# Bands of 192 keys from the second group's pairs on, and the seventh group's second product as seven of quarters

## The chip, the cores and the metric

One Trainium2 chip, one of its cores. The metric is the device time of one execution in microseconds (us), lower is better. The core has a matrix engine (TensorE: PE in the profile, its weight loads PEld), VectorE (DVE), ScalarE (ACT), GpSimd (POOL) and a queue that issues DMA transfers (SyncE: SP).

## The reference

```python
def _attn_ref(q, k, v):                       # 8 batches, 8 heads, 576 positions, 64 wide
    window = 128
    scores = scale * np.matmul(q, k.transpose(0, 1, 3, 2))
    bias = slopes[:, None, None] * (-np.abs(rel).astype(np.float32))[None, :, :]
    mask = (rel >= 0) & (rel < window)
    scores = np.where(mask, scores + bias[None], -1000000000.0)
    scores = scores - np.max(scores, axis=-1, keepdims=True)
    attn = np.exp(scores)
    attn = attn / (np.sum(attn, axis=-1, keepdims=True) + 1e-09)
    return np.matmul(attn, v).astype(np.float32)

def _moe_ref(x, w_in, w_out):                 # 4608 tokens, 512 wide, 2048 hidden
    h = x @ w_in
    g = h * (1.0 / (1.0 + np.exp(-h)))
    return (g @ w_out).astype(np.float32)
```

A query sees itself and the 127 keys before it. The output of attention, its heads side by side, goes through two dense layers with a SiLU between them.

## The kernel before

**Tiles.** The 4608 tokens are 36 tiles of 128, and four tiles are one of nine groups of 512 (numbered 0 to 8; the seventh is group 6). Attention works in 72 **pairs**: pair p is tile p // 2 with half of the heads (four of them). Two batches make nine tiles, so that in every ninth tile (block 0) there are no earlier keys.

**A pair** goes through `scores` (TensorE, queries times keys), `other_batch` (a fill where a tile spans two batches), `row_max` (VectorE: scores plus the bias table `tab`, and the row's extreme), `exps` (ScalarE), `p_hi` and `p_lo` (the weights as two fp16 parts in a buffer `hr`, made by ScalarE and by GpSimd or VectorE), `p_transpose` (DMA transposes from `hr` to `hl`), `attend` (TensorE, weights times values) and `normalize`, `x_hi`, `x_lo`. Queries of a tile reach 128 keys of the tile before and 128 of their own. `banded(p)` says how the keys are cut. Not banded, all 128 queries are multiplied with all 256 keys. Banded, the first 64 queries take the first 192 keys of the 256, the last 64 queries the last 192, so each row has 192 scores (`WIN`). Before, pairs 36 to 71 are banded; their queries and keys are fp16 in two parts, three products for each score. Pairs 8 to 35 are not banded, and their queries and keys are fp32. Pairs 0 to 7 belong to group 0 and run ahead of the dense layers.

**The dense layers.** Each group has 16 steps n (n = 16 times the group, plus f). A step has a first product (`gemm1`, tag h), the activation in parts `act1` (ScalarE), `act2` (VectorE), `act3` (ScalarE) and `act4` (VectorE), and a second product (`gemm2`, tag o). From group 2 on, all operands are fp16 in two parts, three matmuls for each product. Groups in `FAST` take the second product as seven products of quarters (`gemm2_fast`, tag m) in place of eight: for each step `act_sums` makes three more sums of quarters of the activation, and `act3` and `act4` then work on seven quarters in place of four. The sums of weights that this needs are made on GpSimd far ahead (`SUM_WORK`); from step 120 on the first product is made of sevens too (`gemm1_seven`), with sums of the first weights (`IN_WORK`), kept in DRAM meanwhile. When half of a fast group is through, `join_products` adds the products up and stores the result. Before, FAST holds groups 7 and 8.

**The order.** It is written by hand. A step has four positions: the two halves of `gemm1` and the two halves of an earlier step's `gemm2` (how much earlier says `lag_of`: one step in groups 0 to 5, rising to three towards a fast group, three and four in it). At each position `begin()` runs what `put`, `later` and `ahead` have planned for it, so the place of each instruction on its engine is fixed when the kernel is built. `at(p)` gives the position of a pair's scores, 7 apart from pair 18 on; `attend` follows 11 to 19 positions later. Engines work down their own queues in order.

**Buffers.** Not banded, each half of a pair takes one of two `hr` buffers. Banded, all pairs share one buffer (`room`, with gaps of zeros that `clear_room` sets once), and two transposes send it out when both halves are in it. PSUM gives two banks to tag h, two to tag a (scores, attend), and one each to w, x, y, z (second product).

Of the kernel before, what the change touches and what calls it, by code (L numbers as in the profile page):

```python
# [117 lines left out]
SUM_TAGS = tuple(f"w1_{k}" for k in range(7, 15))  # L118
# [34 lines left out]
def tile_window_attention_then_silu_mlp(ctx, tc, qk, v, w_in, w_out, distance, out):  # L153
# [212 lines left out]
    def rescale_bias(b):  # L366

        ratio = vsc[b][:, 8:9] if b > QK16 else vsc[b][:, 7:8]
        for s in range(2):
            off = HALF * s if b == QK16 else 0  # L370
            nc.vector.tensor_scalar_mul(
                tab[halves[s], :, :WIN], tab[halves[s], :, off : off + WIN], ratio[halves[s]]
            )
# [249 lines left out]
    def split_of(p, u, what):  # L623
        if banded(p):
            parts = what[:, HALF:].rearrange("p (u a h c) -> p u a h c", u=2, a=2, h=2)
            return parts[:, u, :, :, :WIN]
        n = 2 - blocks(p).start
        return what[:, : 4 * n * P].rearrange("p (a h c) -> p a h c", a=2, h=2)

    def p_hi(p, u):  # L630
        t, n = st[p]["t"][u], (2 - blocks(p).start) * P
        if banded(p):
            st[p]["hr", u] = hr = room[0]
            nc.scalar.copy(split_of(p, u, hr)[:, 0], t)  # L634
            return
# [1044 lines left out]
```

## Time and profile before

| | us |
|---|---|
| median of 3 runs (897.73 to 897.88) | 897.84 |
| the profiled execution | 896.72 |
| its span, first to last instruction | 894.9 |
| PE busy | 886.3 (99%) |
| DVE busy | 647.4 (72%) |
| ACT busy | 589.1 (66%) |
| POOL busy | 418.5 (47%) |

Busy time of a matmul contains a modelled end, and matmuls overlap. What a stretch of matmuls costs is therefore read below from the start of one stretch to the start of the next, not from the busy time of its instructions. An fp32 matmul of scores leaves two records in the trace, an fp16 one a single record.

### The profile page before, as it was taken

To read this page: it belongs to the slowest core of one execution; us is meant where nothing else is said; L and a number is where in the kernel's file an instruction comes from. 1 tells how busy PE (TensorE), PEld (TensorE's weight loads), DVE (VectorE), ACT (ScalarE), POOL (GpSimd) and SP (SyncE) were. 2 spreads that over 40 slices of the span, in tenths; PEclk is the share of its full clock that TensorE was granted. 3 is DMA by queue.
4 is the path that set the end of the run, shared out by engine and by line. 5 is a ranking of instruction groups with operands and counts; after the bars stand their busy time and mean duration, and the time that the engine had idled before them with its cause. 6 is when DMAs were issued, how large, how long until landed. Compare 5 with 4: busy or idle time off the path is not lost.

```text
span 894.9 us, 22095 instructions
## 1 busy us (share of the span) xinstructions
PE 886.3 (99%) x8617; PEld 589.6 (66%) x8617; DVE 647.4 (72%) x1654; ACT 589.1 (66%) x1321; POOL 418.5 (47%) x494
## 2 busy tenths in 40 slices
PE   9999999999999999999999999999999999999998
PEld 7877777888855555445455554445555568899997
DVE  6997988678876766655777667575776659776665
ACT  7789987776578855777765555565566554465653
POOL 2356651112112211666676776686777412443441
PEclk9999999999999999999999999999999999999999
DMA  8979925345588744869885557565575455400000
GB/s 322 399 191 263 244 56 134 72 95 96 117 216 220 191 96 119 179 163 225 188 155 108 109 105 154 123 118 109 125 166 95 84 85 142 142 26 13 14 25 26
DMA packets 207193, 123.22 MB, mean 138 GB/s; under 512 B 170864, under 2 KB 173040, under 8 KB 207088
## 3 DMA queue, kind: packets, MB, share of 16 engines
q1 hardware_dynamic: 206656, 121.41, 56.7%
q8 instruction: 68, 1.11, 0.5%
q10 hardware_dynamic: 432, 0.39, 0.1%
q14 instruction: 37, 0.30, 0.1%
HBM read 66.72 MB, written 13.63 MB: 90 GB/s over the span
## 4 chain that ended last, share of the span: by engine, by line
PE 79%; DVE 8%; ACT 5%; DMA 3%; POOL 3%; issue 2%; SPq 1%; DVEq 0%; POOLq 0%; ACTq 0%
PE o L1248 26%; PE h L1032 22%; PE m L1151 7%; PE h L1037 5%; PE sp L535 4%; PE av L713 4%; PE h L975 3%; PE hb L975 3%; PE sp L556 2%; PE av L699 1%; ACT t L613 1%; DMA qs<-qk 1%; SPq L664 1%; DMA vm<-v 1%; PE pt L678 1%
## 5 line engine op out<-in xcount | busy, mean ns | idle before, releaser
L1032 PE MATMUL h<-xt,w 128*128 128x512 f16 (+1 forms) x1344 | 269.0, 349 | 0.0
L1248 PE MATMUL o<-w,gb 128*128 128x512 f16 x960 | 224.4, 379 | 0.8 <-DVE gb L1120 0.6
L1032 PEld LDWEIGHTS <-w 128*128 128x128 f16 x1344 | 126.6, 98 | 111.7 <-issue 3.3
L1071 DVE SCALAR_TENSOR_TENSOR h<-gt,h 128x512 f32<-128x512 f32 x112 | 77.6, 693 | 127.2 <-ACT gt L1065 126.6
L1248 PEld LDWEIGHTS <-gb 128*128 128x128 f16 x960 | 90.2, 98 | 104.9 <-DVE gb L1120 2.6
L1065 ACT ACTIVATE gt<-h,tsc 128x512 f32<-128x512 f32 x104 | 71.1, 683 | 112.7 <-PE h L1032 105.2
L202 POOL TENSOR_TENSOR hr<-t,hr 128x384 f16<-128x384 f32 (+2 forms) x54 | 55.9, 1036 | 127.7 <-ACT hr L634 64.4
L202 POOL TENSOR_TENSOR x<-xs,x 128x256 f16<-128x256 f32 x54 | 37.3, 690 | 160.3 <-ACT x L752 151.1
L1248 PE MATMUL o<-w,gh 128*128 128x512 f32 x256 | 82.9, 405 | 0.1
L1106 ACT ACTIVATE gb<-h 128x512 f16<-128x512 f32 x80 | 47.4, 592 | 35.5 <-DVE h L1071 35.2
L613 ACT ACTIVATE t<-t,mx,vsc 128x192 f32<-128x192 f32 x144 | 69.0, 537 | 1.2
L1120 DVE SCALAR_TENSOR_TENSOR gb<-h,gb 128x512 f16<-128x512 f32 x80 | 54.8, 685 | 18.7 <-ACT gb L1106 18.6
L613 ACT ACTIVATE t<-t,mx 128x256 f32<-128x256 f32 (+1 forms) x144 | 61.8, 488 | 3.6 <-DVE mx L598 2.7
L713 PEld LDWEIGHTS <-hl 128*128 128x128 f16 x1464 | 51.8, 98 | 14.6 <-issue 3.9
L713 PE MATMUL av<-v,hl 128*128 128x65 f16 (+1 forms) x1464 | 54.9, 193 | 0.1
L1083 POOL TENSOR_TENSOR gt<-gt 128x256 f32<-128x256 f32 x27 | 21.4, 794 | 68.5 <-DVE gt L1074 68.5
L1248 PEld LDWEIGHTS o<-w,gh 128*128 128x128 f32 x256 | 45.6, 188 | 10.0 <-issue 0.5
L598 DVE CUSTOM_DVE_ANT_0 t<-sp,tab 128x256 f32<-128x256 f32 (+1 forms) x144 | 50.1, 402 | 1.9 <-PE sp L535 1.7
L1248 PE MATMUL o<-w,gl 128*128 128x512 f32 x128 | 50.7, 396 | 0.2
L980 ACT COPY hs<-h 128x128 f32<-128x128 f32 x72 | 19.0, 264 | 41.7 <-PE h L975 38.9
L204 DVE SCALAR_TENSOR_TENSOR hr<-t,hr 128x384 f16<-128x384 f32 (+2 forms) x54 | 42.8, 792 | 5.0 <-ACT hr L634 3.8
L202 POOL TENSOR_TENSOR w<-wm,w 128x512 fp32r<-128x512 f32 x32 | 43.7, 1366 | 2.5
(236 smaller groups left out, 1835.2 us busy)
## 6 DMA issues: line engine op xcount, KB each, us to landing
qs<-qk SPq DMA_DIRECT2D x18, 512.0 KB, 4.6
r<-qk SPq DMA_DIRECT2D x18, 512.0 KB, 4.5
wr<-w_in SPq DMA_DIRECT2D x16, 512.0 KB, 6.5
wr<-w_out SPq DMA_DIRECT2D x16, 512.0 KB, 6.2
rv<-v SPq DMA_DIRECT2D x30, 256.0 KB, 3.6
out<-ot SPq DMA_DIRECT2D x28, 256.0 KB, 2.4
vm<-v SPq DMA_DIRECT2D x27, 256.0 KB, 4.4
q<-qk SPq DMA_DIRECT2D x18, 256.0 KB, 3.4
```

Source lines behind the costliest of these rows:

```text
L202: engine.tensor_sub(out, a, b)
L598: nc.vector.tensor_tensor_reduce(out=st[p]["t"][u][:, h, 2 * P - n :], in0=st[p]["sp"][h][:, u, o].rearrange("p o c -> p (o c)"), in1=tab[ ...
L613: nc.scalar.activation(x, x, AF.Exp, bias=mx[:, 2 * u + h : 2 * u + h + 1], scale=scale)
L713: nc.tensor.matmul(av[:, 2 * u + h, : rhs.shape[-1]], lhs, rhs, start=(n == 0), stop=(n == len(seq) - 1), skip_group_check=True,)
L975: nc.tensor.matmul(h[to], w_of(j, w, a, cc), x_of(g, t, x, b, cc), start=w in ("11", "S1") and i == 0, stop=i == len(terms) - 1, skip_grou ...
L1032: nc.tensor.matmul(o, w[:, wp, cc], x, start=start and k == 0, stop=stop, skip_group_check=True)
L1065: nc.scalar.activation(gt, hps[n], AF.Tanh, scale=scale)
L1071: nc.vector.scalar_tensor_tensor(out=h, in0=gt, scalar=1.0, in1=h, op0=ALU.add, op1=ALU.mult)
L1106: nc.scalar.activation(gh, gt, AF.Copy, scale=cut_of(n))
L1120: nc.vector.scalar_tensor_tensor(out=gl, in0=gt, scalar=cut_of(n), in1=f32(gh) if n // NF < OUT16 else gh, op0=ALU.mult, op1=ALU.subtract)
L1151: nc.tensor.matmul(product(k), a[:, k], sum_part(k, j, part), start=j == 0 and side == 0 and a is gh and part == 0, stop=n == last and a i ...
L1248: nc.tensor.matmul(ops[ti], a[:, t], w, start=(f == 0 and i == 0), stop=(f == NF - 1 and i == len(seq) - 1), skip_group_check=True,)
```

## The change

1. `banded(p)` holds from pair 8 on. `scores_banded` gets a form with a single fp32 product for pairs 8 to 35. `row_max`, `exps`, `p_hi`, `p_lo`, `p_transpose` of these 28 pairs work on 192 keys; all share the one `hr` buffer, which is cleared at the start (position -18), and `p_transpose` is called once a pair. The bias table is shifted for the second half of the queries by a copy of its own (`shift_bias`, position -16) and no longer when it is first rescaled.
2. `FAST` holds group 6 too. Its `act_sums` run on GpSimd, two positions after `act2` (`SUM_LATE`). Its first product is cut into matmuls of 256 columns, as in the other fast groups. The lag of three steps is reached in group 5.
3. The GpSimd work on sums of weights starts earlier and runs denser (`SUMS` 172 in steps of 25; it was 200 in steps of 28), so that it ends before group 6.
4. Places: pairs 10 to 14 one or two positions later (`CLOSE`), the attends of pairs 21 to 35 at 18 positions behind the scores, of pairs 9 to 17 one position sooner, `act3` and `act4` of group 7 one position later, sums of group 7 on GpSimd from step 114 (was 116). Buffers: the cleared buffer has the tag hr, the joined sums of group 7 and 8 take their turn in it.

```diff
-SUMS, SUMS_STEP = 200, 28
+SUMS, SUMS_STEP = 172, 25
-HR_CLEAR = 150
+HR_CLEAR = -18
+SHIFT = -16
-FAST = (NG - 2, NG - 1)
+FAST = (NG - 3, NG - 2, NG - 1)
-CLOSE = (-6, 5, 8, 14, 20, 26, 32, 38)
+CLOSE = (-6, 5, 10, 15, 21, 27, 32, 38)
...
     def banded(p):
-        return p >= 2 * QK16 * NBLK
+        return p >= 2 * GT
...
-                for n, (a, b) in enumerate(((0, 0), (1, 0), (0, 1))):
+                terms = ((0, 0), (1, 0), (0, 1)) if i >= QK16 * NBLK else ((None, None),)
+                for n, (a, b) in enumerate(terms):
...
+                            lhs = qs[i][rows, 2 * q + u, halves[s]] if a is None else q16[i][rows, a, 2 * q + u, halves[s]]
+                            rhs = ks[k][rows, 2 * q + u, keys] if a is None else k16[k][rows, b, 2 * q + u, keys]
                             nc.tensor.matmul(
-                                sp[h][halves[s], u, at4 : at4 + keys.stop - keys.start],
-                                q16[i][rows, a, 2 * q + u, halves[s]], k16[k][rows, b, 2 * q + u, keys],
-                                start=n == 0, stop=n == 2, skip_group_check=True,
+                                sp[h][halves[s], u, at4 : at4 + keys.stop - keys.start], lhs, rhs,
+                                start=n == 0, stop=n == len(terms) - 1, skip_group_check=True,
                             )
...
-        st[p]["hr", u] = hr = pool.tile([P, 8 * P], F16, tag="hr", bufs=2, name=f"hr{p}_{u}")
...
-        nc.sync.dma_start_transpose(hl[:, : 4 * n], hr[:, : 4 * n * P])
...
-        act_sums(n)
+        if n >= ALONE * NF or not SUM_LATE:
+            act_sums(n)
...
+                            if g in FAST and g < ALONE and SUM_LATE:
+                                ahead(1 + SUM_LATE, act_sums, n)
```

The rows below stand as the two programs have them, engine by engine. First TensorE at pair 20, in group 1: sp is the scores, k the keys of the earlier and of the own tile, q the queries. Before, the whole pair:

```order
L535 MATMUL sp_0_2483<-k_1582,q_2016 128x128
L535 MATMUL sp_1_2484<-k_1582,q_2016 128x128
L535 MATMUL sp_0_2483<-k_2018,q_2016 128x128
L535 MATMUL sp_1_2484<-k_2018,q_2016 128x128
L535 MATMUL sp_0_2483<-k_1582,q_2016 128x128
L535 MATMUL sp_1_2484<-k_1582,q_2016 128x128
L535 MATMUL sp_0_2483<-k_2018,q_2016 128x128
L535 MATMUL sp_1_2484<-k_2018,q_2016 128x128
```

TensorE at the same place in the changed kernel, half of the pair (the other half reads the same):

```order
L563 MATMUL sp_0_2559<-k_1637,q_2082 64x128
L563 MATMUL sp_1_2560<-k_1637,q_2082 64x128
L563 MATMUL sp_0_2559<-k_2084,q_2082 64x128
L563 MATMUL sp_1_2560<-k_2084,q_2082 64x128
L563 MATMUL sp_0_2559<-k_2084,q_2082 64x64
L563 MATMUL sp_1_2560<-k_2084,q_2082 64x64
L563 MATMUL sp_0_2559<-k_1637,q_2082 64x64
L563 MATMUL sp_1_2560<-k_1637,q_2082 64x64
```

Eight matmuls of 128 queries and 128 keys became sixteen of 64 queries and 128 or 64 keys. Next TensorE in the second product of step 101 in group 6 (gb: the activation's two parts, w: a weight, o: an output tile). Before, one half of its 12 matmuls:

```order
L1248 LDWEIGHTS gb_9899
L1248 MATMUL o_0_9543<-w_1_2_3479,gb_9899 128x512
L1248 LDWEIGHTS gb_9899
L1248 MATMUL o_0_9543<-w_1_2_3479,gb_9899 128x512
L1248 LDWEIGHTS gb_9899
L1248 MATMUL o_0_9543<-w_1_2_3479,gb_9899 128x512
```

TensorE in the changed kernel, the same step, the first six of its 21 matmuls (m: a bank with two products, ws: sums of weights, gt: the activation's first part):

```order
L1141 LDWEIGHTS gt_10292
L1141 MATMUL m_0_1_9890<-w_1_6_4338,gt_10292 128x256
L1141 LDWEIGHTS gt_10292
L1141 MATMUL m_0_1_9890<-w_1_6_4338,gt_10292 128x256
L1141 LDWEIGHTS gt_10292
L1141 MATMUL m_0_1_9890<-w_1_2_3565,gt_10292 128x256
L1141 LDWEIGHTS gt_10292
L1141 MATMUL m_0_1_9890<-w_1_2_3565,gt_10292 128x256
L1141 LDWEIGHTS gt_10292
L1141 MATMUL m_0_3_9895<-ws_7753,gt_10292 128x256
L1141 LDWEIGHTS gt_10292
L1141 MATMUL m_0_3_9895<-ws_7753,gt_10292 128x256
```

Twelve matmuls of 512 columns became 21 of 256. Last GpSimd in group 6, from pair 64's p_lo on (hr) to the next pair's (x: attention's output in two parts, v: values, wr, wq, ws: sums of weights). Before:

```order
L202 TENSOR_TENSOR hr_0_4009<-t_0_9695,hr_0_4009 128x2x192
L807 TENSOR_TENSOR wr_9728<-w_1_7_4364 128x512
L816 TENSOR_TENSOR wq_9851<-wr_9728 128x256
L817 TENSOR_TENSOR wq_9851<-wr_9728 128x256
L202 TENSOR_TENSOR x_9871<-xs_9773,x_9871 128x256
L504 TENSOR_SCALAR v_69<-rv_9703,vsc_7153 128x8x64
L819 TENSOR_TENSOR wq_9851<-wr_9728 128x256
L820 TENSOR_TENSOR wq_9851<-wr_9728 128x256
L834 CAST ws_9891<-wq_9851 128x2x256
L822 TENSOR_TENSOR wr_9728<-wr_9728 128x256
```

GpSimd in the changed kernel, the same pair on (gt: sums of the activation's quarters):

```order
L207 TENSOR_TENSOR hr_0_528<-t_0_9972,hr_0_528 128x2x192
L1073 TENSOR_TENSOR gt_10016<-gt_10016 128x256
L1074 TENSOR_TENSOR gt_10016<-gt_10016 128x256
L1075 TENSOR_TENSOR gt_10016<-gt_10016 128x128
L207 TENSOR_TENSOR x_10193<-xs_10076,x_10193 128x256
L1073 TENSOR_TENSOR gt_10115<-gt_10115 128x256
L1074 TENSOR_TENSOR gt_10115<-gt_10115 128x256
L1075 TENSOR_TENSOR gt_10115<-gt_10115 128x128
L508 TENSOR_SCALAR v_69<-rv_9983,vsc_7382 128x8x64
L207 TENSOR_TENSOR hr_0_528<-t_0_10187,hr_0_528 128x2x192
```

The sums of weights are gone from group 6, and three sums for each step stand in their place.

## Rows read from the trace of the kernel before

**Rows 1.** The page: span, busy time by engine.

```profile
span 894.9 us, 22095 instructions
...
PE 886.3 (99%) x8617; PEld 589.6 (66%) x8617; DVE 647.4 (72%) x1654; ACT 589.1 (66%) x1321; POOL 418.5 (47%) x494
```

**Rows 2.** Who TensorE waited for: us in total, times, longest.

```profile
PE warm L224 <- POOL ident masks.py:199: 1.3, 1, 1.3
PE hb L975 <- DMA wy<-away: 0.6, 2, 0.4
...
PE pt L678 <- ACT t L613: 0.3, 1, 0.3
```

**Rows 3.** TensorE in time order: start us, busy us, line, shapes, records. fp32 pairs.

```profile
149.35 0.71 PE L535 MATMUL sp<-k,q 64*128 64x128 f32 x8
149.99 1.27 PE L1032 MATMUL h<-xt,w 128*128 128x256 f16 x10
...
228.87 1.16 PE L535 MATMUL sp<-k,q 64*128 64x128 f32 x16
229.96 1.48 PE L1032 MATMUL h<-xt,w 128*128 128x256 f16 x12
```

**Rows 4.** TensorE in time order: an fp16 banded pair.

```profile
374.39 0.72 PE L556 MATMUL sp<-packed,packed 64*64 64x128 f16 x48
375.04 2.76 PE L1248 MATMUL o<-w,gb 128*128 128x512 f16 x12
```

**Rows 5.** TensorE in time order: fp32 matmuls 65 columns wide.

```profile
29.13 3.68 PE L699 MATMUL av<-vf,hl 128*128 128x65 f32 x32
32.65 1.92 PE L767 MATMUL xp<-ident,early 128*128 128x128 f32 x16
```

**Rows 6.** TensorE in time order: a second product in group 6.

```profile
646.81 2.75 PE L1248 MATMUL o<-w,gb 128*128 128x512 f16 x12
649.40 0.88 PE L713 MATMUL av<-v,hl 128*128 128x65 f16 x24
```

**Rows 7.** TensorE in time order: first and second product in group 7.

```profile
754.15 0.60 PE L1151 MATMUL m<-w,gt 128*128 128x256 f16 x4
...
756.44 2.78 PE L1004 MATMUL h<-xt,w 128*128 128x256 f16 x24
759.06 0.60 PE L1151 MATMUL m<-w,gh 128*128 128x256 f16 x4
```

**Rows 8.** Windows, groups 0 and 6: length, busy PE, PEld, DVE, ACT, POOL, clock, DMA.

```profile
35.60:146.60 111.00, 110.64 (x754) 86.60 (x752) 96.23 (x239) 95.78 (x210) 60.45 (x62) 1.00 0.73 195
640.90:728.50 87.60, 87.60 (x973) 44.49 (x971) 57.72 (x153) 51.95 (x106) 49.06 (x56) 1.00 0.57 115
```

**Rows 9.** VectorE by line and shape, 652 to 747 us: busy us, mean ns, idle.

```profile
L1120 DVE SCALAR_TENSOR_TENSOR gb<-h,gb 128x512 f16<-128x512 f32 x14 | 9.6, 685 | 2.5 <-ACT gb L1106 2.4
```

**Rows 10.** VectorE and GpSimd by line and shape, 775 to 880 us.

```profile
L1113 DVE SCALAR_TENSOR_TENSOR gl<-gt,gh 128x640 f16<-128x640 f32 x12 | 9.9, 823 | 0.0
L1113 DVE SCALAR_TENSOR_TENSOR gl<-gt,gh 128x256 f16<-128x256 f32 x12 | 6.6, 548 | 0.0
L1083 POOL TENSOR_TENSOR gt<-gt 128x256 f32<-128x256 f32 x22 | 16.5, 752 | 55.4 <-DVE gt L1074 55.4
...
L1085 POOL TENSOR_TENSOR gt<-gt 128x128 f32<-128x128 f32 x23 | 12.8, 558 | 1.8
```

**Rows 11.** VectorE and GpSimd in time order, group 7: start us, busy us.

```profile
762.58 0.84 POOL L1083 TENSOR_TENSOR gt<-gt 128x256 f32<-128x256 f32 x1 [2.96 <-DVE gt L1074]
762.76 2.21 DVE L1113 SCALAR_TENSOR_TENSOR gl<-gt,gh 128x640 f16<-128x640 f32 x2
763.38 1.30 POOL L1084 TENSOR_TENSOR gt<-gt 128x256 f32<-128x256 f32 x1
```

**Rows 12.** DMA issues, 40 to 100 us, and ScalarE's wait on them, 36 to 150 us.

```profile
hl<-hr SPq DMA_TRANSPOSE x12, 3.6
...
ACT hr L638 <- DMA hl<-hr: 2.1, 2, 1.7
```

More of the change, by code (lines that the diff above doesn't have):

```diff
@@ L117 @@
 OUT_TAGS = {3: ("q", 2), 4: ("q", 2), 5: ("q", 2), 6: ("q", 2)}
[L118 removed]
+SUM_TAGS = tuple(f"w1_{k}" for k in (7, 8, 9, 14, 10, 11, 12, 13))
 MORE_TAGS = (("w1_15", 1), ("k", KSLOTS), ("k", KSLOTS))
@@ L368, in rescale_bias, with shift_bias @@
         ratio = vsc[b][:, 8:9] if b > QK16 else vsc[b][:, 7:8]
[L369 to L373, printed above, removed]
+        nc.vector.tensor_scalar_mul(tab[:, :, :WIN], tab[:, :, :WIN], ratio)
+    def shift_bias():
+        nc.vector.tensor_copy(tab[halves[1], :, :WIN], tab[halves[1], :, HALF:])
     def scale_of(squares, name, spare_bits, scale, inv):
@@ L593, in row_max @@
             return
-        for u, h in [(k, 0), (k, 1)] if p < 2 * GT else [(0, k), (1, k)]:
+        for u, h in [(k, 0), (k, 1)]:
             if u not in st[p]["t"]:
-                tag, bufs = ("x", 4) if 2 * GT < p < 4 * GT and p % 2 and u else ("t", 3)
-                st[p]["t"][u] = pool.tile([P, 2, 2 * P], F32, tag=tag, bufs=bufs, name=f"t{p}_{u}")
+                st[p]["t"][u] = pool.tile([P, 2, 2 * P], F32, tag="t", bufs=3, name=f"t{p}_{u}")
             nc.vector.tensor_tensor_reduce(
@@ L621, in clear_room, with split_of @@
         nc.gpsimd.memset(r[:, 16 * P :], 0.0)
[L623 to L628, printed above, removed]
-    def p_hi(p, u):
[L631 to L635, printed above, removed]
-        st[p]["hr", u] = hr = pool.tile([P, 8 * P], F16, tag="hr", bufs=2, name=f"hr{p}_{u}")
+    def split_of(u):
+        parts = room[0][:, HALF:].rearrange("p (u a h c) -> p u a h c", u=2, a=2, h=2)
+        return parts[:, u, :, :, :WIN]
@@ L646, in p_lo, with p_transpose @@
             return
         nc.vector.scalar_tensor_tensor(
[L648 removed]
+            out=hr[:, 1], in0=t, scalar=PSCALE, in1=hr[:, 0], op0=ALU.mult, op1=ALU.subtract
         )
[L651 to L668 removed]
+    def p_transpose(p):
+        tag, bufs = ("hl", 2)
+        if ATTEND_BAND > 12 and p >= LONG_FROM and p % 3 == 2:
+            tag, bufs = HL_TAGS.get(p, HL_TAG), 1
+        both = pool.tile([P, 2, 8, P], F16, tag=tag, bufs=bufs, name=f"hl{p}")
+        st[p]["hl"] = {u: both[:, u] for u in range(2)}
+        for s in range(2):
+            off = HALF * (1 - s)
+            nc.sync.dma_start_transpose(
+                both.rearrange("p u a c -> p (u a) c")[:, :, halves[s]], room[0][halves[s], off : off + 16 * P]
+            )
@@ L969, in gemm1_seven @@
             hps[n] = [ps_of("h", f"h{n}"), ps_of("wy"[n % 2], f"hb{n}")]
-            hsum[n] = pool.tile([P, 4, P], F32, tag="hr", bufs=2, name=f"hs{n}")
+            if not hsum:
+                hsum["all"] = pool.tile([P, 2, 4, P], F32, tag="hr", bufs=1, name="hs")
+            hsum[n] = hsum["all"][:, n % 2]
         h = [a[:, k * P : (k + 1) * P] for a in hps[n] for k in range(2)]
@@ L1404, in tile_window_attention_then_silu_mlp @@
             for u in range(2):
-                put(4, p_hi, p, u)
-                put(6, p_lo, p, u)
-                put(6, p_transpose, p, u)
+                put(P8[0], p_hi, p, u)
+                put(P8[1], p_lo, p, u)
+            put(P8[1], p_transpose, p)
         elif p < 2 * GT:
@@ L1424, in tile_window_attention_then_silu_mlp @@
                 put(n + 4 + late + u * (1 + more), p_lo, p, u)
-                put(n + 4 + late + u * (1 + more), p_transpose, p, u)
+            put(n + 5 + late + more, p_transpose, p)
         put(a, attend, p)
```

71 lines of the change are left out of this document (28 added, 43 removed).

## The prediction

> **What bounds the kernel now.** I read the page first. TensorE is busy for 886.3 of the 894.9 us of the span, and the other engines are busy for 47 to 72% [rows 1]; its clock is granted in full, the 2.4 GHz level, in group 0 and in group 6 [rows 8]. Busy time of TensorE holds modelled ends, so I went on to the list of what TensorE waited for: five entries, 1.3 us before the first matmul and four between 0.3 and 0.6 us [rows 2]. And in time order one stretch of matmuls begins where the one before has run out. So the kernel is one long row of matmuls, and nothing else is late. A change is worth here what it takes out of TensorE's row, less what it makes TensorE wait; relief of VectorE, ScalarE or GpSimd is worth nothing, and a load on them costs only when it comes through to TensorE.
>
> **The scores of pairs 8 to 35.** An fp32 pair takes 229.96 - 228.87 = 1.09 us of the row for 16 records; a first pair of a batch, with its own tile's keys alone, takes 0.64 us for 8 [rows 3]. So eight records cost 0.45 us and the rest, 0.20 us, is paid once for each pair (filling and emptying at the change of shape). The two heads of a record pair work side by side, in the two halves of the array's rows: four steps in 0.45 us, 0.112 us a step of 128 keys.
>
> In the new form a step holds four matmuls, two heads and two halves of queries. No fp32 matmul of the trace is cut in this way; the fp16 bands of pairs 36 to 71 are. Their 48 records take 0.65 us [rows 4]. 24 fp16 matmuls of 256 columns take 2.62 us [rows 7], 0.055 for each 128 columns. If the four matmuls of a step run together, the fp16 band has six steps of 128 keys and six of 64, 6 x 0.055 + 6 x 0.027 = 0.49 us, and 0.16 us are left for filling and emptying. If they did not, it would need 1.0 us. So in fp16 they run together. The fp32 pair then has, for each two heads, two steps of 128 keys and two of 64: 2 x (2 x 0.112 + 2 x 0.056) = 0.67 us, and with 0.16 to 0.20 us around it 0.83 to 0.87 us. I take 0.85 us, the fp32 row's 0.20 us less something, since a load of 64 columns should be the shorter one. The saving is 1.09 - 0.85 = 0.24 us in 26 pairs, **6.2 us**; pairs 18 and 19 (first of a batch) stay at about 0.64 us and count as nothing. The ends for the range: 0.83 us a pair gives 6.8 us, and a step that costs 0.112 us whatever its keys gives nothing (below).
>
> **The other work of these pairs** shrinks with the keys: bias and maximum, exponentials and both fp16 parts handle 192 columns in place of 256. It lies beside TensorE's row and counts as nothing. The values' products (24 matmuls) stay.
>
> **One buffer instead of two.** p_hi of a pair now waits until both transposes of the pair before have landed, and behind it in ScalarE's queue stand the activations on which TensorE depends. A transposition takes 3.6 us at the median while weights are loading [rows 12], and p_hi and p_lo stand before it. Pairs in group 0 are five positions or more apart; 64 positions take 111 us there [rows 8], so five are 8.7 us, and 5 us remain for p_hi and p_lo, four short instructions. ScalarE waited 2.1 us on this already, without a wait of TensorE there [rows 2, 12]. ScalarE and VectorE are busy for 96 of 111 us in group 0 [rows 8]; the smaller pairs give room. I take zero, and up to 2 us for the range. The copy that shifts the bias and the clearing lie ahead of pair 8 and are single instructions; zero.
>
> **Group 6's products.** A second product takes 649.40 - 646.81 = 2.59 us now [rows 6]. As sevens it takes 756.44 - 754.15 = 2.29 us [rows 7], 16 x 0.30 = **4.8 us less**. The first product is cut into 256 columns: 759.06 - 756.44 = 2.62 us [rows 7] in place of twelve matmuls of 512 columns, 2.59 us as the second product; 16 x 0.03 = 0.5 us more. Together 4.3 us less.
>
> **What group 6 pays beside TensorE.** VectorE: act4 takes 0.82 + 0.55 us for seven quarters [rows 10] in place of 0.69 [rows 9], 16 x 0.68 = 11 us on 57.7 us [rows 8]: 69 of 87.6 - 4.3 = 83 us, and a few joins at the half and at the end. GpSimd: the three sums take 2 x 0.75 + 0.56 = 2.06 us [rows 10], 33 us for 16 steps; but the sums of weights, seven of the ten instructions shown ahead for GpSimd, leave the group. I take it that as much leaves as comes, and that GpSimd stays near its 49 us [rows 8]. Step by step there is time: act4 is planned eight positions after the first product, its second product thirteen, about five positions or 6 us of cover. The places where cover is thin are the half and the end of the group, where banks w to z must be emptied through VectorE while one first product (2.62 us) runs. I take 1.0 us in all, some two waits like those of [rows 2], and keep 0 to 4 us. The earlier sums of weights make GpSimd denser in groups 3 to 5; of the pairs there only p_lo and x_lo wait on it, and from pair 21 on the attends stand 18 positions behind the scores. Zero.
>
> **The sum.** -6.2 - 4.3 + 1.0 = -9.5 us. The profiled execution took 896.72 us (1.8 us around its span), so 887.2 us; the median of the runs lies 1.1 us above it, so **888.3 us**.
>
> **The rivals.**
>
> *A step costs its load (no gain from the bands).* For it: fp32 matmuls only 65 columns wide take 32.65 - 29.13 = 3.52 us for 32 records, 0.110 us each, as much as 128 columns [rows 5]; there the load of 128 columns sets the pace. If it is the same with 64, eight steps at 0.112 and 0.20 make 1.09 us, the old price: 888.3 + 6.2 = 894.5 us. Against it: the loads are half as wide here, and the fp16 band shows 0.027 us for a step of four loads of 64. 9%. The Trainium skill, TensorEngine Tiling (Array Packing), Performance Considerations, speaks in the same direction: each matmul carries some 60 cycles, so that splitting a dimension that is already short gains nothing. As an estimate from it, eight more matmuls at 25 ns would take 0.2 us of the 0.24 back, 893.5 us; the trace does not agree, since 48 records in 0.65 us are 14 ns each [rows 4].
>
> *The halves of queries run one after the other in fp32 (slower).* Then the steps double: 2 x 0.67 + 0.20 = 1.54 us a pair, 0.45 us more in 26 pairs, +11.7 us in place of -6.2: 906.2 us. It decides from 1.29 us a pair on: there the pairs' loss is 5.2 us, which covers the 3.3 us that group 6 brings and 0.2% more. For it: no fp32 row has four parts, and two records in sequence make up each fp32 matmul. Against it: heads already run side by side in fp32 [rows 3], four parts in fp16 [rows 4]. 6%.
>
> *VectorE becomes the bound in group 6.* Where GpSimd's sums ran at the same time, the two parts of act4 took 2.21 us, and the sum beside them 1.30 us in place of 0.75 [rows 10, 11]. At that price act4 adds 16 x 1.52 = 24 us, 82 of 83 us, and with VectorE's waits for ScalarE and GpSimd in between it would run some 4 us behind TensorE: 888.3 + 4 = 892 us, the single buffer's waits included. For it: joins, scores' maxima and sums meet in one group for the first time. Against it: GpSimd is busy for little more than half of the group, so that only a part of the act4 meets it, and the 6 us of cover. 25%, of which 5 are for a price of 8 us and more. The Trainium skill, GPSIMD Engine Reference, Specifications, says that GpSimd shares its way into SBUF with VectorE and that VectorE's instructions with two SBUF inputs contend with it; act4 is one of these, and the two prices (1.37 us on average, 2.21 us beside a sum) agree.
>
> **How the numbers follow.** The forecast, both gains in full within some 2 us, gets 56%; VectorE's rival 25%, the bands without gain 9%, the halves in sequence 6%, and 4% a time under the range. The range reaches from 885.0 us (0.83 us a pair and no wait give 886.7, and 1.7 us that I don't foresee) to 894.5 us; it takes in VectorE's rival up to 6 us (20 of its 25%) and, for less than 80% would be held without it, half of the bands without gain, which may come out on either side of 894.5: 81% in all. 0.2% of the time, 1.8 us, is about what a measurement can tell from no change; it puts faster under 896.0 us. Faster: 56, 9 and 4%, and 20 of VectorE's 25, so 0.89; of the other 5 I put 4 with the same, 0.04, and 1 with the halves in sequence, slower 0.07.
>
> **What would show it.** Right: in the profile of the changed kernel a pair of groups 1 and 2 takes 0.83 to 0.87 us from the start of its scores to the next stretch; second products of group 6 take 2.29 us; TensorE's waits stay under 5 us. The bands' rival would show 1.09 us a pair, the slower one 1.5. VectorE's rival shows gaps in front of group 6's second products, ended by act4, by a join or by the emptying of a bank, and VectorE busy for over 90% there. A wait of TensorE on an activation in group 0, with ScalarE held up by a transposition in front of it, would prove the single buffer's price wrong.

## The result, and the profile after

The changed kernel takes 905.40 us (median of 5 runs, 904.58 to 906.71), the kernel before 897.84 us on the same chip: 1.0088 times the time before, 95% interval 1.0074 to 1.0101. It is slower, where 888.3 us (885.0 to 894.5) was forecast. The profiled execution took 905.13 us, its span is 903.3 us.

First the page of the changed kernel, beside [rows 1], then the list of TensorE's waits (us in total, times, longest), beside [rows 2]:

```profile
span 903.3 us, 23781 instructions
...
PE 879.8 (97%) x9385; PEld 617.3 (68%) x9385; DVE 651.8 (72%) x1682; ACT 585.4 (65%) x1337; POOL 457.6 (51%) x548
```

```profile
PE av L700 <- DVE mx L595: 4.4, 4, 2.1
PE o L1238 <- ACT gb L1096: 3.5, 3, 1.7
PE hb L964 <- DMA wy<-away: 2.1, 2, 1.2
PE sp L563 <- DVE xs L729: 1.5, 2, 0.9
PE warm L229 <- POOL ident masks.py:199: 1.3, 1, 1.3
PE m L1141 <- DVE xs L729: 1.3, 2, 1.1
```

TensorE has less to do than before (879.8 us against 886.3), and it waits: the whole list holds 15 entries and 18.6 us, before it was 3.3 us. The forecast had added 1.0 us to that.

What the change was to take out of TensorE's row is gone from it. In time order (start us, busy us, line, shapes, records) a banded fp32 pair, beside [rows 3], and a second product of group 6, beside [rows 6, 7]:

```profile
231.10 0.90 PE L563 MATMUL sp<-k,q 64*64 64x128 f32 x32
231.93 1.48 PE L1021 MATMUL h<-xt,w 128*128 128x256 f16 x12
...
713.79 0.61 PE L1141 MATMUL m<-w,gt 128*128 128x256 f16 x4
...
716.09 2.78 PE L993 MATMUL h<-xt,w 128*128 128x256 f16 x24
```

A pair takes 231.93 - 231.10 = 0.83 us in place of 1.09, the second product 716.09 - 713.79 = 2.30 us in place of 2.59.

So the question is where the waits lie. For that I took, from the time order of TensorE in each trace, the start of the first product of each step, and how far it stands behind the same step of the kernel before. The table holds this for the changed kernel and for those of the experiments (us; negative is ahead). From step 81 to 111 single steps can't be compared where group 6 is taken as sevens, because the step's second product moved against the first one; at 80 and from 112 on they can.

| step | 6 | 8 | 12 | 48 | 64 | 80 | 112 | 120 | 124 |
|---|---|---|---|---|---|---|---|---|---|
| changed kernel | 0.8 | 4.2 | 4.4 | 1.0 | 9.5 | 9.5 | 5.6 | 6.2 | 8.2 |
| e1 bands alone | 0.2 | 5.5 | 5.7 | 2.7 | 3.7 | 3.7 | 2.9 | 3.0 | 2.7 |
| e2 sums early alone | 1.1 | 1.1 | 1.1 | 1.8 | 6.9 | 6.9 | 6.9 | 6.9 | 7.0 |
| e3 second buffer | 0.8 | 1.4 | 1.6 | -1.6 | 4.0 | 4.0 | 0.1 | 0.8 | 4.3 |
| e4 late reductions | 0.2 | 5.0 | 5.3 | 2.8 | 2.0 | 2.0 | -2.0 | -1.3 | 2.2 |
| e5 old places | 4.0 | 3.7 | 3.2 | 1.8 | 8.4 | 8.4 | 4.6 | 5.3 | 7.1 |
| c1 e3 and e4 | 0.8 | 1.4 | 1.6 | -1.8 | -3.0 | -3.0 | -6.9 | -6.3 | -2.7 |
| c2 and exchanged buffers | 0.8 | 1.4 | 1.6 | -0.7 | -1.8 | -1.8 | -5.8 | -5.1 | -5.6 |
| c3 and near attends | 0.3 | 0.9 | 1.1 | 0.1 | -1.8 | -1.8 | -5.6 | -4.9 | -5.4 |
| d1 stores later | 1.2 | 6.1 | 6.3 | 3.6 | 10.0 | 10.0 | 6.0 | 6.7 | 10.1 |
| d3 c2, sums of group 7 earlier | 0.2 | 0.7 | 0.9 | -1.3 | -2.4 | -2.4 | -6.4 | -5.0 | -6.0 |
| d4 d3 and d1 | 0.3 | 0.9 | 1.1 | -1.4 | -0.8 | -0.8 | -4.8 | -3.4 | -4.4 |

The changed kernel, e1, e4 and d1 have the same program in group 0 and stand 4.4 to 6.3 us behind at step 12: by so much single traces differ, so differences along one row are safer than those between rows. Three places lose in the changed kernel: steps 6 to 8 in group 0 (3.4 us), steps 48 to 64 in group 3 (8.5 us), and step 121 (2 us). In between it gains: 3.4 us from step 12 to 48, and from step 80 to 112, that is mainly in group 6, 9.5 - 5.6 = 3.9 us. Inside the first of these gains lie small waits: from 147 to 356 us, in groups 1 and 2, TensorE waits for 3.0 us in all, where the kernel before has no wait.

**Group 0.** Rows of TensorE, VectorE and ScalarE in time order; the last column is the time that the engine stood still before, and what ended it:

```profile
82.63 0.53 ACT L635 ACTIVATE hr<-t 128x384 f16<-128x384 f32 x1 [0.84 <-DMA hl<-hr]
83.18 0.56 DVE L642 SCALAR_TENSOR_TENSOR hr<-t,hr 128x384 f16<-128x384 f32 x1 [0.63 <-ACT hr L635]
...
84.21 0.90 PE L563 MATMUL sp<-k,q 64*64 64x128 f32 x32
...
88.45 0.42 DVE L209 SCALAR_TENSOR_TENSOR x<-xs,x 128x256 f16<-128x256 f32 x1 [1.67 <-ACT x L739]
89.39 0.35 DVE L595 CUSTOM_DVE_ANT_0 t<-sp,tab 128x192 f32<-128x192 f32 x1
...
90.17 0.88 PE L700 MATMUL av<-v,hl 128*128 128x65 f16 x24 [2.07 <-DVE mx L595]
```

Read from below: at 90.17 the attend of pair 11 waits 2.07 us for a bank of tag a; both are held by the scores of pair 13 (84.21) until `row_max` has read them. `row_max` (89.39) is late because VectorE, which works in order, stood 0.63 us for the p_hi that ScalarE makes, and ScalarE had stood for the transposition out of the single buffer (82.63); VectorE then stood 1.67 us for the x of an earlier pair, which ScalarE makes too. These stands add up: from 36 to 125 us ScalarE waits 3.8 us for `hl<-hr` and VectorE 3.6 us for p_hi. With a second buffer (e3, below) the first is gone and the second 1.1 us, while the wait for x is still 1.70 us, so it is not what the single buffer adds. The same chain, with 1.30 us at TensorE, stands at 79.13.

**Group 3.** SyncE's queue, ScalarE and TensorE, 361 to 372 us (`away<-wx` is the store of a sum of first weights, vm and qs are loads for the statistics of batches 6 and 7):

```profile
361.25 0.91 SPq L855 DMA_DIRECT2D away<-wx  x2
362.20 0.48 SPq L260 DMA_DIRECT2D vm<-v  x1
362.73 0.58 SPq L280 DMA_DIRECT2D qs<-qk  x1
365.42 4.79 SPq L654 DMA_TRANSPOSE hl<-hr  x2
...
369.03 0.63 ACT L274 ACTIVATE vm<-vm 128x512 f32<-128x512 f32 x1 [4.12 <-DMA vm<-v]
369.65 0.67 ACT L1054 ACTIVATE gt<-h,tsc 128x512 f32<-128x512 f32 x1
...
371.74 1.76 PE L1238 MATMUL o<-w,gb 128*128 128x512 f16 x6 [1.44 <-ACT gb L1096]
```

ScalarE stands 4.12 us on a reduction whose load has not landed. Behind it in its queue stands `act1` (369.65), and so the second product waits. Before, no store of a sum stood ahead of these two loads (358.42 and 358.90 there). At 408 to 424 us it happens again, with qs (ScalarE stands 3.01 us, TensorE 1.74), and there the clock falls too (last section). In between ScalarE stands for a load that has no store just ahead of it, but a transposition:

```profile
391.50 3.22 SPq L654 DMA_TRANSPOSE hl<-hr  x2
394.77 1.16 SPq L260 DMA_DIRECT2D vm<-v  x1
...
399.44 0.63 ACT L274 ACTIVATE vm<-vm 128x512 f32<-128x512 f32 x1 [2.90 <-DMA vm<-v]
```

And the kernel before has one store of a sum right ahead of two such loads (404.00, then 405.36 and 406.24), for which ScalarE doesn't stand. So here a store ahead is neither needed for the wait nor enough for it.

**Step 121** waits for a sum of first weights that comes back from DRAM:

```profile
781.94 0.29 PE L964 MATMUL hb<-xs,wy 128*128 128x128 f16 x2 [1.20 <-DMA wy<-away]
783.12 0.40 PE L964 MATMUL hb<-xs,wy 128*128 128x128 f16 x4 [0.89 <-DMA wy<-away]
```

### The profile page after: what moved, and what is told of

Read it like the earlier page. It is cut to its first block, busy times and chain, and to the rows that moved or that the text cites. A ratio compares the mean times of both kernels' runs of the same rounds, so it can differ in the third digit from the quotient of the medians.

```text
span 903.3 us, 23781 instructions
## 1 busy us (share of the span) xinstructions
PE 879.8 (97%) x9385; PEld 617.3 (68%) x9385; DVE 651.8 (72%) x1682; ACT 585.4 (65%) x1337; POOL 457.6 (51%) x548
## 4 chain that ended last, share of the span: by engine, by line
PE 63%; DMA 11%; DVE 10%; ACT 6%; POOL 4%; SPq 3%; issue 2%; DVEq 0%; ACTq 0%; POOLq 0%
PE o L1238 19%; PE h L1021 15%; PE m L1141 9%; PE h L993 4%; PE h L964 3%; PE sp L563 3%; PE av L700 3%; PE h L1026 3%; DMA hl<-hr 3%; PE hb L964 3%; DMA vm<-v 2%; DMA qs<-qk 2%; SPq L654 2%; DMA wr<-w_out 2%; ACT gt L1054 1%
## 5 line engine op out<-in xcount | busy, mean ns | idle before, releaser
L1021 PE MATMUL h<-xt,w 128*128 128x512 f16 (+1 forms) x1152 | 224.3, 344 | 0.0
L1238 PE MATMUL o<-w,gb 128*128 128x512 f16 x768 | 181.2, 381 | 4.5 <-ACT gb L1096 3.5
L1021 PEld LDWEIGHTS <-w 128*128 128x128 f16 x1152 | 108.2, 98 | 90.9 <-issue 3.7
L1238 PEld LDWEIGHTS <-gb 128*128 128x128 f16 x768 | 71.9, 98 | 88.9 <-ACT gb L1096 5.0
L207 POOL TENSOR_TENSOR hr<-t,hr 128x384 f16<-128x384 f32 x54 | 53.1, 983 | 102.0 <-ACT hr L635 96.1
L1073 POOL TENSOR_TENSOR gt<-gt 128x256 f32<-128x256 f32 x45 | 38.4, 854 | 91.5 <-DVE gt L1063 91.5
L595 DVE CUSTOM_DVE_ANT_0 t<-sp,tab 128x192 f32<-128x192 f32 x256 | 75.4, 348 | 1.1 <-PE sp L563 1.1
L635 ACT ACTIVATE hr<-t 128x384 f16<-128x384 f32 x128 | 63.1, 512 | 10.7 <-DMA hl<-hr 10.5
L993 PE MATMUL h<-xt,w 128*128 128x256 f16 x576 | 67.7, 273 | 0.0
L700 PEld LDWEIGHTS <-hl 128*128 128x128 f16 x1464 | 52.5, 98 | 18.8 <-issue 10.1
L619 ACT ACTIVATE t<-t,mx 128x192 f32<-128x192 f32 (+2 forms) x144 | 56.6, 452 | 5.0 <-DVE mx L595 3.1
L993 PEld LDWEIGHTS <-w 128*128 128x128 f16 x576 | 55.2, 98 | 6.5
L1238 PEld LDWEIGHTS o<-w,gh 128*128 128x128 f32 x256 | 45.8, 188 | 10.1 <-DVE vsc L327 1.2
```

The lines of the kernel that those rows point to most:

```text
L207: engine.tensor_sub(out, a, b)
L595: nc.vector.tensor_tensor_reduce(out=st[p]["t"][u][:, k], in0=st[p]["sp"][k][:, u], in1=tab[:, 4 * q + 2 * u + k, :WIN], scale=scale, scal ...
L619: nc.scalar.activation(x, x, AF.Exp, bias=mx[:, 2 * u + h : 2 * u + h + 1], scale=scale)
L635: nc.scalar.activation(split_of(u)[:, 0], st[p]["t"][u], AF.Copy, scale=scale)
L700: nc.tensor.matmul(av[:, 2 * u + h, : rhs.shape[-1]], lhs, rhs, start=(n == 0), stop=(n == len(seq) - 1), skip_group_check=True,)
L993: nc.tensor.matmul(out, w[:, wp, cc], xt[g, "g"][:, 2 * t : 2 * t + 2, xp * NCC + cc], start=half == 0 and i == 0, stop=i == len(seq) - 1, ...
```

## The experiments

Each set had its own runs of the kernel before (medians 897.4, 897.4 and 897.2 us). The ratios are to these.

| kernel | us | ratio to before, 95% interval |
|---|---|---|
| e1_bands | 898.38 | 1.0007 (0.9997 to 1.0016) |
| e2_sums | 903.59 | 1.0067 (1.0052 to 1.0082) |
| e3_rooms | 901.03 | 1.0039 (1.0024 to 1.0054) |
| e4_reduce | 898.33 | 1.0010 (1.0001 to 1.0019) |
| c1_both | 894.28 | 0.9964 (0.9951 to 0.9977) |
| c2_back | 891.06 | 0.9924 (0.9907 to 0.9940) |
| c3_close | 892.29 | 0.9944 (0.9929 to 0.9958) |
| c4_before_reduce | 896.19 | 0.9987 (0.9977 to 0.9996) |
| d1_stores | 905.23 | 1.0089 (1.0067 to 1.0111) |
| d3_x7 | 890.46 | 0.9925 (0.9909 to 0.9940) |
| d4_all | 892.51 | 0.9950 (0.9938 to 0.9963) |
| e5_places | 902.97 | 1.0064 (1.0050 to 1.0078) |

### The parts apart: bands alone, early sums alone

```diff
-SUMS, SUMS_STEP = 172, 25
+SUMS, SUMS_STEP = 200, 28
-FAST = (NG - 3, NG - 2, NG - 1)
+FAST = (NG - 2, NG - 1)
```

(e1, on the changed kernel; with it the places and buffers of the sums and of group 7 as before.)

> Bands from pair 8 on, the single buffer and the places of the changed kernel; group 6 takes its second product as eight again, and the sums of weights start where they did before (200, steps of 28). Theory (two losses: the single buffer in group 0, about 4 us; the earlier sums of weights in group 3, about 8.5 us): group 0 still loses about 4 us by step 8, the start of step 48 stands about 1 us after that of the kernel before, and group 3 no longer loses, so that the end comes 0 to 2 us before it: 896 to 898 us. Rival (group 3 loses because of the bands, not because of the sums): step 64 starts some 9 us late as in the changed kernel, and without group 6's 4 us the time is 908 us or more.

Measured 898.38 us, just above what the theory gave and not to be told from the kernel before. Group 0 loses 5.5 us, group 3 only 1.0 (2.7 at step 48, 3.7 at 64). So the bands and their single buffer bring 6.8 us in shorter pairs and lose it again, most of it in group 0: TensorE waits for 4.7 us there and for 3.4 us in groups 1 and 2, and the kernel before for nothing. They are not what makes group 3 lose.

```diff
-SUMS, SUMS_STEP = 200, 28
+SUMS, SUMS_STEP = 172, 25
```

(e2, on the kernel before; with it the sums of first weights at 131 and 16 positions behind the others.)

> The kernel before, with nothing changed but the places of the sums of weights (172 in steps of 25, the sums of first weights at 131 and 16 behind, the buffers they need). Theory: the stores of the sums of first weights stand ahead of the statistics' loads of the last two batches in the queue, ScalarE waits for these loads with the activations behind it, and group 3 loses 6 to 9 us: 904 to 907 us. Rival (the bands make group 3 lose): 897 to 899 us.

Measured 903.59 us, and from step 48 to 64 the loss grows from 1.8 to 6.9 us. The earlier sums alone make group 3 lose, a little less than in the theory. ScalarE's waits on DMA at 355 to 432 us:

```profile
ACT qs L284 <- DMA qs<-qk: 3.7, 1, 3.7
ACT vm L269 <- DMA vm<-v: 3.6, 3, 1.8
```

Before it was 2.8 and 2.7 us there, without a wait of TensorE on an activation's first part. TensorE's longest wait in e2 comes behind this stretch, again with a stand of ScalarE before it, and here VectorE's part of the activation is late:

```profile
436.01 0.63 ACT L284 ACTIVATE qs<-qs 128x512 f32<-128x512 f32 x1 [2.42 <-DMA qs<-qk]
...
443.43 2.33 PE L1248 MATMUL o<-w,gb 128*128 128x512 f16 x10 [2.09 <-DVE gb L1120]
```

### Each loss repaired by itself

```diff
+TWO = (9, 11, 13)
...
-        room[0] = r = pool.tile([P, HALF + 16 * P], F16, tag="hr", bufs=1, name="hr0_0")
+        tag, bufs = ("big", 2) if k else ("hr", 1)
+        room[k] = r = pool.tile([P, HALF + 16 * P], F16, tag=tag, bufs=bufs, name=f"hr{k}_0")
```

> The changed kernel with a second buffer for the weights' parts of pairs 9, 11 and 13 (it takes a turn in a buffer that nothing else uses before step 11). Theory: p_hi in group 0 no longer waits for the transposition of the pair before, ScalarE and VectorE run earlier, and most of the 3.4 us between steps 6 and 8 comes back: 905.4 - 3 = 902.4 us. Rival (the new places of pairs 10 to 14, with one position less between the scores of pair 13 and the attend of pair 11, make TensorE wait for the bank): 905.4 us within 1.

Measured 901.03 us, 4.4 less than the changed kernel. From step 6 to 8 the loss is 0.6 us in place of 3.4, and ScalarE's wait for `hl<-hr` in group 0 (3.8 us in the changed kernel, 2.1 before, [rows 12]) is gone; TensorE's wait for `mx` falls from 3.6 to 0.9 us.

```diff
-            put(n + 4, vscale_reduce, b, i)
-            put(n + 6, qk_sum, b, i, 0)
-            put(n + 7, qk_sum, b, i, 1)
+            late = 3 * (b == 3)
+            put(n + 4 + late, vscale_reduce, b, i)
+            put(n + 6 + late, qk_sum, b, i, 0)
+            put(n + 7 + late, qk_sum, b, i, 1)
```

> The changed kernel with the three reductions of each step of the last two batches' statistics three positions later (7, 9 and 10 behind their loads in place of 4, 6 and 7). Theory: in group 3 ScalarE no longer stands on these loads, TensorE's waits there (steps 50 to 60) go, and step 64 starts within 2 us of the kernel before in place of 9.5 us behind: 905.4 - 7.5 = 898 us. Rival (the transfers crowd out the transposes too, or the sums of weights on GpSimd are what delays): 903 us or more.

Measured 898.33 us, 7.1 less than the changed kernel. TensorE waits for nothing from 352 to 470 us, and from step 48 to 64 it gains 0.8 us where the changed kernel lost 8.5.

The rival on group 0, that the new places make the wait:

```diff
-CLOSE = (-6, 5, 10, 15, 21, 27, 32, 38)
+CLOSE = (-6, 5, 8, 14, 20, 26, 32, 38)
-A8, A9, A10 = 17, 13, 14
+A8, A9, A10 = 17, 12, 15
```

> The changed kernel with the places of pairs 9 to 17 as before the change (pairs 10 to 13 one or two positions earlier, their attends where they were), single buffer. Theory (the single buffer makes group 0's loss, the places do not): group 0 still loses 3 us or more by step 12, and pairs that follow closer on one another make p_hi wait longer: 905 to 908 us. Rival (the places make it): step 12 within 1.5 us of the kernel before, 902 us.

(The places of pairs 10 to 13 change; pair 14 stands at 32 in both kernels.) Measured 902.97 us: my number (905 to 908) missed, the rival's time came nearly. But group 0 has lost 3.2 us by step 12, as the theory said, only elsewhere. ScalarE and TensorE at that place:

```profile
62.16 0.52 ACT L635 ACTIVATE hr<-t 128x384 f16<-128x384 f32 x1 [5.66 <-DMA hl<-hr]
...
65.90 0.70 PE L1238 MATMUL o<-w,gh 128*128 128x512 f32 x2 [1.77 <-ACT gh L1092]
```

With pair 10 three positions behind pair 9, ScalarE stands 5.66 us for the single buffer, and TensorE waits for the activation behind it, the sign that the prediction names. With the later places it stands less at a time, but the attend of pair 11 comes two positions behind the scores of pair 13 in place of three. The buffer is the cause (e3), the places choose where it shows; of the two the old ones cost some 1 us less by step 12 and 2.4 us less in the end.

### The repairs together

> The changed kernel with both repairs, the second buffer in group 0 and the later reductions of the last two batches' statistics. Theory (the two losses are separate): 905.4 - 4.4 - 7.1 = 893.9 us, so faster than before by 3.5 us. Rival (both come from one lateness of ScalarE, so that the second repair finds less): 896 us or more.

Measured 894.28 us: the two losses add up.

```diff
-IN_TAGS = {... 1: ("w1_4", 1), ... 4: ("w1_5", 1), ...}
-IN_BACK = {4: 470, ... 1: 472}
+IN_TAGS = {... 1: ("w1_5", 1), ... 4: ("w1_4", 1), ...}
+IN_BACK = {1: 470, ... 4: 472}
```

> c1_both, and the sums of first weights for step 121 come back into the buffer that was meant for step 124's and the other way round, with their places in the queue exchanged too. Theory: step 121's load stood in the queue behind VectorE's last sum of group 8's activations, which VectorE, busy all the time at the start of group 7, made late; now it doesn't wait for it, and the 2.0 us of TensorE's waits at step 121 go, with the lower clock that followed: 3 to 3.5 us less than c1_both, 890.5 us. Rival (the queue stands there anyway, and steps 124 to 126 wait instead): within 1 us of c1_both.

Measured 891.06 us, 0.9924 of the kernel before (0.9907 to 0.9940). From step 120 to 124 the kernel now gains 0.5 us, where c1_both lost 3.6. SyncE's queue still waits for VectorE as long as ever, the row of c2_back here from 735 to 800 us,

```profile
SPq L875 <- DVE xs L210: 11.3, 2, 7.4
```

(11.9 us in the changed kernel), but nothing that step 121 needs stands behind it. The page of c2_back and the five longest of its TensorE waits:

```profile
span 889.5 us, 23790 instructions
...
PE 875.7 (98%) x9385; PEld 617.1 (69%) x9385; DVE 658.0 (74%) x1682; ACT 584.4 (66%) x1337; POOL 457.3 (51%) x550
```

```profile
PE warm L230 <- POOL ident masks.py:199: 1.3, 1, 1.3
PE m L1146 <- DVE xs L734: 1.3, 2, 1.1
PE sp L564 <- DVE xs L734: 1.2, 1, 1.2
PE av L705 <- DVE mx L596: 1.0, 2, 0.7
PE vt L340 <- DVE mx L596: 0.9, 1, 0.9
```

TensorE is busy 10.6 us less than before, and the list of its waits holds 9.2 us against 3.3.

```diff
-ATTEND_BAND, LONG_FROM = 18, 21
+ATTEND_BAND, LONG_FROM = 18, 36
```

> c2_back, with the attends of pairs 21 to 35 at 11 positions behind their scores again, as in the kernel before. Theory: the small waits of groups 1 and 2 for a bank (statistics' column products and scores, some 2.4 us together with none before) come from the attends' new place behind the next pair's scores, and half or more go: 1 to 2 us less than c2_back. Rival (they come from VectorE's time, or the nearer attends wait for their transposition out of the single buffer): the same as c2_back or slower.

Measured 892.29 us, no gain. The wait of scores for xs goes, a new one of 0.6 us for `hl<-hr` and 1.1 us of attends with no releaser come in its place; those on `mx` and `row` stay, but for 0.9 us at `vt`. The theory falls: with the attends near again the small waits of groups 1 and 2 come to as much (3.5 us from 147 to 355 us, 3.6 in c2_back). What makes them stays open; ScalarE stands for the single buffer there too (2.3 us in c2_back), and no run gave these groups a second one.

> The kernel before with the later reductions alone. Theory: there ScalarE's wait for these loads was covered, so nothing is to be had: 897.4 us within 0.7. Rival (the places of the reductions are worth something by themselves): 895 us or less.

Measured 896.19 us, 0.9987 (0.9977 to 0.9996) of the kernel before: 0.5 us below the stretch that was expected. The kernel before had two waits of TensorE in this stretch, 0.6 us for an activation's second part and 0.5 us for xs; now 0.3 us of the first is left. So 1 us was to be had before as well, and the other 6 of e4's 7 us repair the change's own loss.

### Which part of the early sums delays ScalarE

```diff
-        put(IN_SUMS[j] + IN_AWAY, in_away, j)
+        put(IN_SUMS[j] + IN_AWAY + 2 * (j in (1, 2)), in_away, j)
```

> The changed kernel with the stores of the second and third sums of first weights two positions later, nothing else: in SyncE's queue each now stands behind the two loads of statistics (v and qk) that it stood ahead of. Theory (the order in the queue at these two places makes group 3's loss): step 64 starts 2 to 4 us behind the kernel before in place of 9.5, 905.4 - 6 = 899.5 us. Rival (GpSimd's sums themselves, or the amount of data, delay ScalarE there): 904 us or more.

Measured 905.23 us: a miss. From step 48 to 64 the loss is 6.4 us in place of 8.5. ScalarE's and GpSimd's waits from 350 to 432 us:

```profile
ACT hr L635 <- DMA hl<-hr: 5.0, 3, 2.4
ACT qs L289 <- DMA qs<-qk: 2.9, 2, 1.7
ACT vm L274 <- DMA vm<-v: 1.4, 3, 0.6
...
POOL wq L803 <- DMA away<-wx: 12.1, 2, 7.8
```

The load of vm no longer holds ScalarE (1.4 us; 7.7 from 355 to 432 us in the changed kernel). But the buffer that a store empties is the one into which GpSimd makes the next sum, and GpSimd, which makes the pairs' p_lo and x_lo too, now stands 12.1 us for the stores (6.5 before this edit); ScalarE stands on the transposition in turn. So the order in the queue delays the load of vm, but the time doesn't fall with it, and the 2.1 us less from step 48 to 64 are no more than single traces differ. That ScalarE's stand is what reaches TensorE is shown by e4; how much of the loads' delay belongs to the stores ahead, to transposes (4.79 us for the two at 365.42) and to the amount of data stays open. Over the whole stretch the DMA engines have no more to do than before: from 355 to 432 us they are busy for 0.77 of the time at 180 GB/s, and for 0.82 at 194 GB/s in the kernel before.

Two more kernels on top of the repairs. In d3_x7 the sums of group 7 move, and take another buffer (the edit shows the places alone); d4_all has the stores' edit too:

```diff
-X7, X8, X9 = 448, 456, 464
+X7, X8, X9 = 442, 456, 464
```

> c2_back with the sums of group 7's activations six positions earlier on VectorE (in the buffer that group 8's first sums take next). Theory (VectorE is the bound for some 10 us around the start of group 7, where the joins of group 6's second half meet these sums): the 1.3 us that TensorE waits there for a bank go, 891.1 - 1.3 = 889.8 us. Rival (the wait moves to group 6's last steps, whose activations VectorE now makes later): 891 us within 0.6.

> d3_x7 and d1_stores together, so five repairs in all: second buffer, later reductions, exchanged buffers for steps 121 and 124, earlier sums of group 7, stores behind the loads. Theory: with the reductions later, what the stores' order still costs at steps 48 to 52 is 0.7 us in c2_back; 889 us, 0.990 to 0.992 of the kernel before. Rival (nothing is left there): as d3_x7.

d3_x7: 890.46 us, the same as c2_back. The wait for a bank at the start of group 7 is 1.5 us, not gone: from step 112 to 116 it loses 1.4 us where c2_back lost 0.5, and what it is ahead was gained in groups 0 to 2, which the edit doesn't touch. The rival was right that nothing is to be had there. d4_all: 892.51 us, 2 us more than d3_x7, lost between steps 48 and 64 (it gains 1.2 us there without the stores' edit and loses 0.6 with it), where GpSimd stands 10.1 us for the stores against 5.0 in c2_back. Both theories fell. The best version is c2_back or d3_x7, some 6.5 us under the kernel before and 14 under the changed one.

## Why the prediction was wrong

**TensorE's row: right.** -6.2 - 4.3 = -10.5 us were forecast; with most of the disturbances away (c2_back) TensorE is busy 886.3 - 875.7 = 10.6 us less (11.6 in d3_x7). A pair costs 0.83 us, the low end of what was given, 0.26 x 26 = 6.8 us. The first two rivals, which price the pair at 1.09 and 1.54 us, are out. The estimate by the rule of some 60 cycles for each matmul (the Trainium skill, TensorEngine Tiling (Array Packing), Performance Considerations), which gave nearly no gain for the bands, did not come: the 32 records of the new pair take 0.26 us less than the 16 of the old one.

**"One buffer instead of two ... I take zero, and up to 2 us for the range": wrong, 3.4 to 5.5 us.** The mechanism was named, ScalarE held up by a transposition with TensorE's work behind it, but its cover was reckoned as 8.7 us between pairs less 3.6 for a transposition, as if p_hi and p_lo came at once. ScalarE was busy for 96 of 111 us in group 0 [rows 8], VectorE as long, so p_lo came late, the transposes later still (two in 3.2 to 4.8 us), and ScalarE stood some 0.8 to 1.3 us at a time, four times (5.66 us once in e5_places). The wait did not go to the products alone: it ran through VectorE to the banks of tag a. The second buffer gives back 4.4 us (e3_rooms), where the range had 2. That the 2.1 us of [rows 12] reached no one before was no evidence that more would not.

**"The earlier sums of weights make GpSimd denser ... Zero": wrong, 5 to 8.5 us, the largest error.** The step looked at who waits for GpSimd. It left out that each sum is stored through SyncE's queue, in which the statistics' loads of the last batches stand, and that ScalarE, which works in order, has its reductions four positions behind the loads with `act1` behind them. The wait was in the trace: ScalarE waited 2.8 us for qs and 2.7 us for vm in this stretch before, and c4_before_reduce shows that about 1 us was to be had there already, so it had no slack to lose. What the runs show in place of the zero: the earlier sums alone cost 5.1 us from step 48 to 64 and 6.1 us in the end (e2_sums), ScalarE stands on the loads of the statistics, and reductions three positions later give back 7.1 us (e4_reduce). Through what the sums delay these loads stays open (d1_stores).

**"1.0 us in all" for group 6: right there, short at its end.** From 640 to 736 us TensorE waits for nothing. The window of group 6, with the columns of [rows 8]:

```profile
640.90:734.00 93.10, 93.05 (x1359) 78.92 (x1348) 73.81 (x185) 60.32 (x129) 55.48 (x68) 1.00 0.61 112
```

(It is longer than the 87.6 us of before because the longer lag, reached in group 5, leaves 16 second products in it in place of 13.) VectorE is busy 73.8 of 93.1 us, 79%, short of being the bound. Its `act4`, with GpSimd's sums beside, by line and shape from 650 to 736 us:

```profile
L1103 DVE SCALAR_TENSOR_TENSOR gl<-gt,gh 128x640 f16<-128x640 f32 x8 | 9.5, 1194 | 0.5 <-ACT gh L1083 0.5
L1103 DVE SCALAR_TENSOR_TENSOR io<-gt,gt 128x640 f16<-128x640 f32 x7 | 7.4, 1059 | 0.5 <-DMA out<-ot 0.5
L1103 DVE SCALAR_TENSOR_TENSOR gl<-gt,gh 128x256 f16<-128x256 f32 x8 | 6.6, 825 | 0.0
L1103 DVE SCALAR_TENSOR_TENSOR io<-gt,gt 128x256 f16<-128x256 f32 x7 | 5.0, 707 | 0.0
```

The steps take turns in two buffers, gl and io, and the two parts take 1.19 + 0.83 = 2.02 us in one and 1.06 + 0.71 = 1.77 us in the other, 1.9 us on average: nearer to the rival's 2.21 than to the 1.37 of the forecast's sum [rows 10, 11]. So much of the price of VectorE's rival came, and its consequence did not. The cover held: the shortest distance from the end of an `act4` in group 6 to the first matmul on its result is 6.8 us, in the second step,

```profile
660.34 1.88 DVE L1103 SCALAR_TENSOR_TENSOR io<-gt,gt 128x640 f16<-128x640 f32 x2 [0.45 <-DMA out<-ot]
...
667.98 0.38 PE L1141 MATMUL m<-w,io 128*128 128x256 f16 x2
```

(its second part is at work until 661.16). The joins of group 6's second half, named as a place of thin cover, do reach TensorE at the start of group 7 (1.3 us for a bank).

The clearing and the shift at the start, counted as nothing, can't be seen: the first step starts 1.0 us late in the changed kernel, 0.3 to 1.0 in the others with them, and 0.4 in e2, which has neither there.

**Not in the forecast: step 121, 2 us.** "Places" were read for the pairs alone. The last sums of group 8's activations also moved two positions, and the load for step 121 waits in SyncE's queue for their buffer; c2_back shows it. Before, TensorE waited 0.6 us there. In e1_bands, with these sums and group 6 as before, it is 0.5 us; whether the two positions or group 6's joins on VectorE make the sums late, no run separates. In e3_rooms, e4_reduce, c1_both and d1_stores the clock also falls behind this wait, and steps 120 to 124 lose 3.4 to 3.6 us; in the profile of the changed kernel it stays at 1.00 there.

The account of the profiled execution: 887.2 us were forecast, 905.1 came. 18.6 - 3.3 = 15.3 us of waits stand where 1.0 was put, 14.3 more; and TensorE is busy for 879.8 us where 886.3 - 10.5 = 875.8 was forecast, 4.0 more, of which the lower clock is some 1.7 us (an estimate from 0.83 in the ten us from 420 on, last section); the rest I can't place (c2_back has the same 9385 matmuls in 875.7 us). Together 18.3 us, for a difference of 17.9.

## What to carry to other kernels

Here the edit took out of the bounding engine what its matmul rows said; whether the time followed was decided by the engines that work in order. So for each piece of work that is moved, list its DMAs, the loads that they stand ahead of, and the engine that stands on those loads with the bounding engine's work behind it; a wait that is there already without harm may have no slack left. Where a buffer becomes single, find what stands behind the writer in its queue, and price it with the writer's delays, not with the transfer alone.

## What was not expected of the hardware

After some of the waits TensorE runs slower for a few microseconds. The windows of the changed kernel around the wait at 418.87 (1.74 us); the value before the last two is the granted clock:

```profile
410.00:420.00 10.00, 8.14 (x82) 3.54 (x81) 2.59 (x6) 5.57 (x13) 4.72 (x7) 1.00 0.99 275
420.00:430.00 10.00, 10.00 (x105) 5.20 (x104) 8.19 (x23) 7.33 (x18) 9.06 (x10) 0.83 0.60 167
...
420.50:423.50 3.00, 3.00 (x30) 1.93 (x29) 1.48 (x4) 2.79 (x7) 3.00 (x4) 0.53 0.85 217
```

For 3 us it is 0.53, nearly the lower of the two levels, 1.2 GHz, and the 24 matmuls of an attend there are busy for 1.52 us in place of 0.89 (0.88 in the row at 90.17):

```profile
421.01 1.52 PE L700 MATMUL av<-v,hl 128*128 128x65 f16 x24
```

A wait of TensorE can so cost more than its own length. It does not follow each time: behind the 2.07 us at 90.17 the clock stayed at 1.00 in the changed kernel, and it was 0.83 from 90 to 100 us in the profiles of e1_bands, e4_reduce and d1_stores, which have the same program in group 0. Ten us at 0.83 are some 1.7 us (an estimate), so this makes up much of the spread at step 12 in the table, 4.4 us in the one and 5.3 to 6.3 in the three.
